# One core, packed attention and two gated expert layers: p, k, v attention in front for the first pair of batches alone, the other twelve units between the first pair's expert products

## The chip, the cores and the metric

One core of a Trainium2 chip runs the whole program; nothing is shared with other cores. The metric is the device time in microseconds (us), the median over runs of the same kernel. Five engines work in order, each on its own queue of instructions: TensorE (PE, with its weight loads as PEld), VectorE (DVE), ScalarE (ACT), GpSimd (POOL), and SyncE (SP), whose queue here issues every DMA.

## The reference

Eight batches of eight heads, 576 positions, head size 64, and 32 packed positions `p` per head:

```python
p_packed = sm_attn(p, k, v)                 # 32 packed rows look at 576 keys
out = sm_attn(q, p_packed, p_packed)        # 576 queries look at the 32 packed rows
x = out.transpose(0, 2, 1, 3).reshape(4608, 512)
g = x @ w_gate                              # 512 -> 1536
x = (silu(g) * (x @ w_val)) @ w_out         # 1536 -> 512
a, b = x @ w1, x @ w2                       # 512 -> 1024
return ((a * b) @ w3) @ w_out2              # 1024 -> 1024 -> 512
```

`sm_attn` is a softmax with the maximum taken off and a scale of 1/8. The weights arrive as float64 and are turned into float32 on the chip.

## The kernel before, in words

**Units.** A unit `u` is one batch and half of its heads (four heads), so there are 16. For each unit the first attention runs through `pa_kT` (k and p are transposed on TensorE, ScalarE copies them out), `pa_s` (scores, and VectorE takes their maximum), `pa_exp` (ScalarE), `pa_T` (the exponentials are transposed), `pa_P` (times v, VectorE divides) and `pa_PT` (the packed result is transposed into `PT0` for the first pair of batches, into `PTh` and `PTl` for the later ones).

**Pairs.** Batches are taken in four pairs P. For a pair and each of 12 slices f of the 1536 expert columns, `c_mm` multiplies the packed rows by the slice of `w_gate` and `w_val` (out: `ch`, `cl`, a number kept as two parts). `stage1` multiplies these by the second attention's weights (`aTh`, `aTl`, made by the `q_` functions), takes Silu on ScalarE and the product on VectorE, and splits it into `uh` and `ul`. After each three slices `stage3` multiplies them by `w_out` and adds to `acc`. `stage1` and `stage3` are the expert products that fill TensorE's time.

**Front.** All 16 units, the four q halves of the first pair (`q_rows` to `q_aT`), the conversion of the first weights (`w_conv`, `wo_conv`) and the first two `c_mm` stand ahead of the first `stage1`. The loop over s (L627) puts step s of unit s beside later steps of the units before it; a table (`extra`, L593 to L618) places the q halves and weights among them. This piece is in the written order on every engine. In the loop over pairs and slices (L878) the framework orders the instructions of each engine; that order is fixed once the program is built.

**Weights.** `conv` (L329) turns a raw float64 block into float32: one pass on ScalarE, two or three on VectorE. `raw_load` has three buffers. In pair 0 the slice f+3 of `w` and f+1 of `w_out` are converted while slice f is multiplied; the later pairs read the converted weights back.

**PSUM.** During the front, `psA` has three buffers of two banks and `psB` two of one bank. From slice 0 of pair 0 (`NPS = 0`) all eight banks are one pool `ps` with four buffers of two banks.

Of the kernel before, what the change touches and what calls it, by code (L numbers as in the profile page):

```python
# [16 lines left out]
M0 = None  # L17
KVB = 4
VB = 3
VD = 0  # L20
RAW0 = (2, 2, 4, 7, 10, 13, 14, 16, 17, 19)
WS = {5.0: (0, 0), 7.0: (0, 1), 8.0: (1, 0), 10.25: (1, 1), 15.75: (2, 0), 16.25: (2, 1)}
CVD = (0.25, 1.25)
SPD = 2.25
WO0 = 17.5
CS = (17, 18)
CO = (18.0, 19.0)
QS = (0, 1, 5, 6)
QD = ((0, 'load'), (4.0, 'T'), (5.25, 'mm'), (6.0, 'max'), (6.0, 'sub', 'pool'), (6.75, 'exp'), (7.25, 'sum'), (7.75, 'div', 'pool'), (8.75, 'aT', 'later'), (10.5, 'split'))
STD = 4.75  # L30
W3B = 5
DSIGN = ('w',)
SIGN = -(1 << 31)
W3S = ((0, 1, 2, 3), (1, 3), (1, 3))
NPS = 0
# [3 lines left out]
def packed_attention_moe_kernel(  # L39
# [84 lines left out]
    aA = pool("aA", "left")  # L124
    psA = tc.alloc_tile_pool(name="psA", bufs=3, space=bass.MemoryType.PSUM, reuse_waits="tile")
# [12 lines left out]
    a_pools = [aA, None]  # L138
    hs = [slice(32 * hq, 32 * hq + 32) for hq in range(4)]

    def q_load(b, Q):
        t = qp.tile([128, 2, NB32, 32], F32, tag="qr", name=f"qr{b}_{Q}")
        for i in range(4):
            for pr in range(2):
                nc.sync.dma_start(
                    t[32 * i:32 * i + 32, pr],
                    q[b, 4 * Q + 2 * pr + i // 2, :, 32 * (i % 2):32 * (i % 2) + 32].rearrange(
                        "(n t) d -> t n d", t=32),
                )
        q_t[b, Q] = t  # L150
# [15 lines left out]
    def q_rows(b, Q):  # L166
        t = qp.tile([128, NR, D], F32, tag="qr", name=f"qr{b}_{Q}")
        nc.sync.dma_start(t, q[b, 4 * Q:4 * Q + 4].rearrange("h (p r) d -> (h p) r d", r=NR))
        q_t[b, Q] = t

    def q_rT(b, Q):
        x = q_t.pop((b, Q))
        qT = qp.tile([128, NR // 2, 128], F32, tag="qT", name=f"qT{b}_{Q}")
# [5 lines left out]
        nc.vector.tensor_copy(qT[:, 0:8], t.rearrange("p a (m n) -> p (a m) n", n=128))  # L179
# [3 lines left out]
    def q_rmm(b, Q):  # L183
        qT, PTd = qT_t.pop((b, Q)), PTd_t.pop((b, Q))
        if Q == 0:
            sT_t[b] = qp.tile([128, 2, 2, HS], F32, tag="sT", name=f"sT{b}")
# [39 lines left out]
    def q_max(b, Q=None):  # L226
        sT, n, nj = q_view(b, Q)
        if not Q:
            sm_q[b] = (qp.tile([128, NJ, 1], F32, tag="qmx", name=f"qmx{b}"),
                       qp.tile([128, NJ, 1], F32, tag="qsm", name=f"qsm{b}"))  # L230
# [23 lines left out]
    def q_aT(b, Q, sub_on="dve"):  # L254
        at = a_pools[b // 2 % 2]
        if Q == 0:
            aT_t[b] = (at.tile([128, 2, 2, HS], F32R, tag=f"aTh{b % 2}", name=f"aTh{b}"),
                       at.tile([128, 2, 2, HS], F32R, tag=f"aTl{b % 2}", name=f"aTl{b}"))
        hi, lo = aT_t[b]
        sT = sT_t[b] if Q == 0 else sT_t.pop(b)  # L260
        aT = qp.tile([128, 2, HS], F32, tag="aT", name=f"aT{b}_{Q}")
        nc.vector.transpose(out=aT.rearrange("p a s -> p (a s)"),
                            in_=sT[:, Q].rearrange("p a s -> p (a s)"))
        if sub_on == "later":
# [3 lines left out]
            return conv_q.append(lambda: split(*by_row, src, sub_on="pool"))  # L268
        split(hi[:, Q], lo[:, Q], aT, sub_on=sub_on)

    def q_tasks(b, at, n):
# [46 lines left out]
    def raw_load():  # L318
        if raw_at[0] < len(raw_q):
# [4 lines left out]
            nc.sync.dma_start(t, src)  # L324
            raw_t.append((key, t))

    in_front, conv_rest = [True], []

    def conv(key, t):  # L329
# [13 lines left out]
        dve = not in_front[0] and key.startswith(DSIGN)  # L343
        sg = None if dve else vc.tile(list(t.shape), F32, tag="sg", name=f"sg_{key}")
        nc.vector.tensor_scalar(x, low, 29, None, op0=ALU.logical_shift_right)

        def sign():
            if not dve:
                nc.scalar.activation(sg, high.bitcast(F32), AF.Sign)

        def rest():
            nc.vector.scalar_tensor_tensor(
                x, t.bitcast(I32), 3, x, op0=ALU.logical_shift_left, op1=ALU.bitwise_or)
            if dve:
                nc.vector.scalar_tensor_tensor(
                    t.bitcast(I32), high, SIGN, x, op0=ALU.bitwise_and, op1=ALU.bitwise_or)
            else:
                nc.gpsimd.tensor_tensor(out=t, in0=x.bitcast(F32), in1=sg, op=ALU.mult)

        if in_front[0]:  # L360
            conv_rest.extend((sign, rest))
        else:
            sign()
            rest()
        if not in_front[0]:
            raw_load()
# [40 lines left out]
    wop = pool("wop", "right", bufs=4)  # L407
    cp = pool("cp", "right", bufs=2)
# [66 lines left out]
    def load_kv(u, nm):  # L475
# [30 lines left out]
    def pa_s(u):  # L506
# [10 lines left out]
        mx = pa.tile([128, 1], F32, tag="mx", name=f"mx{u}")  # L517
# [4 lines left out]
    def pa_exp(u, t, mx):  # L522
        a = pa.tile([128, NV, PK], F32, tag="ap", name=f"ap{u}")
# [7 lines left out]
    def pa_T(u):  # L531
# [8 lines left out]
        aT = pa.tile([PK, 2, 3, 128], F32, tag="apT", name=f"apT{u}")  # L540
# [3 lines left out]
    def pa_P(u):  # L544
# [9 lines left out]
        Pz = pa.tile([128, 2, 64], F32, tag="Pz", name=f"Pz{u}")  # L554
# [4 lines left out]
        if u < 4:  # L559
            Pd = pa.tile([128, 2, 64], F32, tag="Pd", name=f"Pd{u}")  # L560
# [4 lines left out]
    def pa_PT(u):  # L565
# [29 lines left out]
    def task(s, fn, *args):
        extra.setdefault(s, []).append((fn, args))

    for (b, Q), s in zip([(0, 0), (0, 1), (1, 0), (1, 1)], QS):
        for d, fn, *x in QD:
            task(s + d, {"load": q_rows, "T": q_rT, "mm": q_rmm, "max": q_max, "sub": q_sub, "exp": q_exp,  # L600
                         "sum": q_sum, "div": q_div, "aT": q_aT,
                         "split": lambda b, Q: conv_q.pop(0)()}[fn], b, Q, *x)
    for s in RAW0:
        task(s, raw_load)
    for s, (f, gv) in WS.items():
        task(s, w_conv, f, gv)
        for d in CVD:
            task(s + d, lambda: conv_rest.pop(0)())
        if gv == 1:
            task(s + STD, w_store, f)  # L610
    task(WO0, wo_conv, 0)
    for d in CVD:
# [499 lines left out]
```

## Time and profile before

| what | value |
|---|---|
| median of 3 runs | 1445.85 us (1436.72, 1446.46, 1445.85) |
| the profiled execution | 1441.93 us; its span is 1440.2 us |
| PE busy in the span | 1393.1 us (97%), 9960 instructions |
| DVE busy | 780.2 us (54%) |
| ACT busy | 642.5 us (45%) |
| POOL busy | 457.7 us (32%) |
| mean granted TensorE clock | 0.98 |
| DMA | 230.26 MB, mean 160 GB/s |

The busy shares are means over stretches with different limits. The profiled execution took 1441.93 us, of which 1440.2 us lie between its first and last instruction; it stands 3.9 us below the median of the runs. A line `L88` is a helper (`sub`) that many steps share, so its rows are told apart by the tiles they name. The span of a matmul in a row includes time in the pipeline; the distance of the starts is what TensorE takes.

### The profile page before, as it was taken

What the parts mean: (1) busy time and instruction counts of PE and PEld (TensorE: products, weight loads), DVE (VectorE), ACT (ScalarE), POOL (GpSimd) and SP (SyncE); (2) the same over time, 40 slices, a digit from 0 to 9 for tenths busy, and PEclk for the clock granted to TensorE, in tenths of its full rate; (3) what the DMA queues carried; (4) which work ended last, traced back from release to release, by engine and by line L of the source; (5) the groups of instructions that cost most, each with busy time, mean ns of one, the idle gap of its engine ahead of it and who ended that gap; (6) DMA issues with size and microseconds to landing.
All of it is one profiled execution on the core that took longest, in us unless ns stands there. A gap on an engine that the chain in (4) does not pass through costs nothing. (4 is left out here: it accounts for less than half of the span.)

```text
span 1440.2 us, 25384 instructions
## 1 busy us (share of the span) xinstructions
PE 1393.1 (97%) x9960; PEld 1302.1 (90%) x9960; DVE 780.2 (54%) x1188; ACT 642.5 (45%) x1077; POOL 457.7 (32%) x341
## 2 busy tenths in 40 slices
PE   7679999999999999999999999999999999999998
PEld 5457998999999999999989999989989899899997
DVE  3467798767875455756366647962333413334130
ACT  5575545536655355564464433643323323233231
POOL 0334133434544434455243223721202112021120
PEclk9888999999999999999999999999999999999999
DMA  9997575676533322215353324964827548275451
GB/s 270 239 248 205 163 210 188 160 237 166 165 83 83 117 60 70 66 53 176 96 157 100 131 72 174 339 242 154 256 75 236 179 133 253 92 223 180 133 168 44
DMA packets 175255, 230.26 MB, mean 160 GB/s; under 512 B 69408, under 2 KB 102176, under 8 KB 175136
## 3 DMA queue, kind: packets, MB, share of 16 engines
q1 hardware_dynamic: 175136, 228.64, 52.2%
q8 instruction: 79, 1.29, 0.4%
q14 instruction: 40, 0.33, 0.1%
HBM read 179.04 MB, written 49.55 MB: 159 GB/s over the span
## 5 line engine op out<-in xcount | busy, mean ns | idle before, releaser
L88 POOL TENSOR_TENSOR ul<-u,uh 128x576 fp32r<-128x576 f32 x96 | 145.4, 1519 | 247.7 <-ACT uh L92 247.3
L1005 POOL TENSOR_TENSOR c<-s,s 128x384 f32<-128x384 f32 x48 | 48.8, 1016 | 376.0 <-ACT s L1000 375.6
L701 PE MATMUL px<-ul,woh 128*128 128x288 f32 x768 | 165.3, 297 | 1.3 <-POOL ul L88 1.3
L701 PE MATMUL px<-uh,woh 128*128 128x288 f32 x768 | 165.4, 297 | 0.7 <-ACT uh L92 0.7
L701 PE MATMUL px<-uh,wol 128*128 128x288 f32 x768 | 164.9, 296 | 0.0
L1000 ACT COPY s<-pA 128x384 f32<-128x384 f32 x144 | 69.0, 479 | 181.1 <-PE pA L985 181.1
L88 DVE TENSOR_TENSOR cl<-pc,ch 64x512 fp32r<-64x512 f32 (+2 forms) x120 | 105.1, 900 | 55.4 <-ACT ch L455 47.6
L701 PEld LDWEIGHTS px<-uh,woh 128*128 128x128 f32 x768 | 124.1, 189 | 2.4 <-issue 1.4
L701 PEld LDWEIGHTS px<-ul,woh 128*128 128x128 f32 x768 | 124.3, 190 | 1.5 <-POOL ul L88 1.5
L701 PEld LDWEIGHTS px<-uh,wol 128*128 128x128 f32 x768 | 124.3, 189 | 0.0
L88 POOL TENSOR_TENSOR wl<-wf,wh 128x1024 fp32r<-128x1024 f32 x36 | 86.9, 2414 | 97.4 <-ACT wh L92 86.7
L1049 PE MATMUL po<-wo_hi,abl 128*128 128x512 f32 x288 | 112.2, 389 | 0.0
L1049 PE MATMUL po<-wo_lo,abh 128*128 128x512 f32 x288 | 112.1, 389 | 0.0
L1049 PE MATMUL po<-wo_hi,abh 128*128 128x512 f32 x288 | 112.0, 389 | 0.0
L711 DVE TENSOR_TENSOR acc<-acc,px 128x576 f32<-128x576 f32 x96 | 71.2, 746 | 66.1 <-PE px L701 65.9
L92 ACT CAST uh<-u 128x576 fp32r<-128x576 f32 x96 | 64.6, 674 | 93.5 <-DVE u L683 93.1
L88 DVE TENSOR_TENSOR abl<-ab,abh 128x768 fp32r<-128x768 f32 x48 | 48.6, 1013 | 105.2 <-ACT abh L92 105.2
L683 DVE TENSOR_TENSOR u<-u,pv 128x576 f32<-128x576 f32 x96 | 72.1, 751 | 48.8 <-PE pv L676 43.2
L88 POOL TENSOR_TENSOR wol<-wof,woh 128x512 fp32r<-128x512 f32 x48 | 66.9, 1406 | 88.3 <-ACT woh L92 80.7
L676 PE MATMUL pg<-aTh,ch 128*128 128x288 f32 x384 | 85.2, 304 | 4.8 <-DVE acc L711 3.3
L681 ACT ACTIVATE u<-pg 128x576 f32<-128x576 f32 x96 | 62.5, 651 | 49.4 <-PE pg L676 46.6
L676 PE MATMUL pg<-aTl,ch 128*128 128x288 f32 x384 | 83.3, 299 | 0.0
(362 smaller groups left out, 3544.1 us busy)
## 6 DMA issues: line engine op xcount, KB each, us to landing
ws<-wsd SPq DMA_DIRECT2D x245, 256.0 KB, 3.1
wf<-Wd SPq DMA_DIRECT2D x36, 512.0 KB, 3.4
raw_w<-in_moe_w_dram SPq DMA_DIRECT2D x32, 512.0 KB, 4.5
wsd<-ws SPq DMA_DIRECT2D x49, 256.0 KB, 4.0
raw_wo<-in_moe_w_out_dram SPq DMA_DIRECT2D x20, 512.0 KB, 4.4
km<-in_k_dram SPq DMA_DIRECT2D x16, 576.0 KB, 8.0
vm<-in_v_dram SPq DMA_DIRECT2D x16, 576.0 KB, 8.0
wof<-wod SPq DMA_DIRECT2D x36, 256.0 KB, 2.8
```

Source lines behind the costliest of these rows:

```text
L88: eng.tensor_tensor(out=out, in0=src, in1=hi.bitcast(F32), op=ALU.subtract)
L92: nc.scalar.copy(hi, src)
L676: nc.tensor.matmul(t[:, hf, 0:HS], lhsT=w[:, b % 2, Q, cols], rhs=x[:, Q, hf, :], start=first, stop=last,)
L681: nc.scalar.activation(u, t[:, :, 0:HS], AF.Silu)
L683: nc.vector.tensor_tensor(out=u, in0=u, in1=t[:, :, 0:HS], op=ALU.mult)
L701: nc.tensor.matmul(t[:, hf, 0:HS], lhsT=w[:, 128 * d:128 * d + 128], rhs=x[:, hf, :], start=first, stop=last,)
L711: nc.vector.tensor_tensor(out=o, in0=o, in1=t[:, :, 0:HS], op=ALU.add)
L1000: nc.scalar.copy(o, t)
L1005: on.tensor_tensor(out=r, in0=o, in1=t, op=op)
L1049: nc.tensor.matmul(t, lhsT=a[:, j, cols], rhs=w[:, f], start=first, stop=last)
```

## The change

The first attention of units 0 to 3 (the first pair of batches) and the first pair's q halves stay in front, in an order written out call by call. The other twelve units are issued by `hook()`: it is called after each `stage1` of pair 0 and after each half of a `stage3` in pair 0, and alternates between two halves of a unit's steps. With it:

- `c_mm` of slices 0 (in front) and 1 (ahead of the first `stage1`) come as before, weights of slices 0 and 1 are converted in front, and slice f+2 is converted while slice f is multiplied (before: f+3).
- In the front, the sign of a converted weight is put in by a third pass on VectorE, not by ScalarE and GpSimd.
- `psA` and `psB` (three buffers of two banks, two of one) stay until slice 10 of pair 0 (`NPS = 10`).
- In every pair, `stage3` of the first batch stands ahead of `stage1` of the next slice (before: behind it); the pools for `u`, k and the second attention's weights are shared or smaller (`up` has 6 buffers for 7).
- The q loads of the later pairs are kept behind the weight load issued before them.

```diff
-NPS = 0
+NFU = 4
+NPS = 10
 ...
+    with tc.manual_schedule(engines=M0):
+        load_p(0)
+        load_kv(0, "k")
+        load_kv(1, "k")
+        load_kv(0, "v")
+        q_rows(0, 0)
 ...
+        front_q(1, 0, "mm")
+        pa_PT(3)
+        front_q(1, 1, "T")
+        c_mm(0, 0)
+        front_q(1, 0, "exp")
+        front_q(1, 1, "mm")
+        w_conv(1, 0)
+        front_q(1, 0, "sum")
+        front_q(1, 1, "exp")
+        front_q(1, 0, "aT")
+        front_q(1, 1, "sum")
+        w_conv(1, 1)
 ...
+    def hook():
+        i, odd = divmod(hook_n[0], 2)
+        hook_n[0] += 1
+        u = NFU + i
 ...
+        if not odd:
+            if on(u):
+                if u % 2 == 0:
+                    twice_p(u // 2)
+                    if u // 2 + 1 < B:
+                        load_p(u // 2 + 1)
+                pa_kT(u)
+                load_kv(u + 3, "k")
+            if on(u - 1):
+                pa_T(u - 1)
+            if on(u - 2):
+                pa_PT(u - 2)
+        else:
+            if on(u):
+                front_s(u)
+            if on(u - 1):
+                pa_P(u - 1)
+                load_kv(u + 1, "v")
 ...
@@ stage3
+            if d % 2 == 1 and P == 0:
+                hook()
@@ the loop over pairs and slices
-        if n > 0 and at(1) is not None:
+        if at(1) is not None:
             c_mm(*at(1))
 ...
+        if pend is not None:
+            stage3(*pend, 0)
+        stage1(2 * P, f)
+        if P == 0:
+            hook()
 ...
+        if pend is not None:
+            stage3(*pend, 1)
+            pend = None
+        stage1(2 * P + 1, f)
+        if P == 0:
+            hook()
```

**The end of the front on TensorE.** Here `pc0_0` and `pc0_1` are the first two `c_mm`, `pg0_0` the first `stage1`; `pat`, `pP`, `pPT` are steps of the units. Before:

```order
L424 MATMUL pc0_0_1568<-wf0_0_452,PT0_79 64x256 x8
L537 MATMUL pat15_1579<-ident_66,ap15_1521 96x128 x6
L551 MATMUL pP14_1588<-vm14_1330,apT14_1519 32x64 x24
L570 MATMUL pPT14_1621<-ident_66,Pz14_1613 128x128
L424 MATMUL pc0_1_1627<-wf0_1_753,PT0_79 64x256 x8
L551 MATMUL pP15_1636<-vm15_1411,apT15_1586 32x64 x24
L570 MATMUL pPT15_1672<-ident_66,Pz15_1661 128x128
L676 MATMUL pg0_0_1702<-aTh0_824,ch0_0_1617 128x288 x2
```

With the change:

```order
L176 MATMUL pqr1_1_596<-ident_66,qr1_1_266 128x128
L402 MATMUL pc0_0_608<-wf0_0_454,PT0_79 64x256 x8
L192 MATMUL psq1_1_622<-qT1_1_594,PTd3_591 32x288 x8
L475 MATMUL pkr4_748<-ident_66,zp2_570 128x128
L478 MATMUL pkr4_748<-ident_66,km4_566 128x128
L475 MATMUL pkr5_888<-ident_66,zp2_570 128x128
L402 MATMUL pc0_1_698<-wf0_1_635,PT0_79 64x256 x8
L696 MATMUL pg0_0_712<-aTh0_403,ch0_0_617 128x288 x2
```

The first expert product no longer follows unit 15 but the last q half of the first pair and `c_mm` of slice 1.

**What `c_mm` of slice 1 waits for on VectorE, with the change.** `wf0_1` is its weight; `qsm1` and `aT1_0` belong to the softmax of the second batch's q halves.

```order
L263 STREAM_TRANSPOSE aT1_0_650<-sT1_572 128x576
L245 TENSOR_REDUCE qsm1_585<-sT1_572 128x18
L246 TENSOR_SCALAR qsm1_585<-qsm1_585 128x18
L247 RECIPROCAL qsm1_585<-qsm1_585 128x18
L341 TENSOR_SCALAR vx_w_1_1_658<-raw_w_1_1_460 128x512
L342 SCALAR_TENSOR_TENSOR vx_w_1_1_658<-wf0_1_635,vx_w_1_1_658 128x512
L344 SCALAR_TENSOR_TENSOR wf0_1_635<-raw_w_1_1_460,vx_w_1_1_658 128x4x128
```

The weight's last pass stands behind the second batch's softmax; before, that weight was ready among the units of the front.

**Slice 1 on ScalarE.** `ch0_2` is the copy of `c_mm` for slice 2, `u0_1` and `u1_1` are the Silu of the two batches, `ap4` is the exponential of unit 4. Before:

```order
L448 CAST ch0_2_1814<-pc0_2_1805 128x1024
L342 ACTIVATE wof0_2_1867<-raw_wo_2_1756 128x512
L681 ACTIVATE u0_1_1818<-pg0_1_1819 128x576
L92 CAST uh0_1_1847<-u0_1_1818 128x576
L92 CAST woh0_2_1924<-wof0_2_1867 128x512
L681 ACTIVATE u1_1_1876<-pg1_1_1877 128x576
```

With the change:

```order
L504 ACT_TABLE_LOAD
L504 ACTIVATE ap4_834,sm4_835<-psp4_822,mx4_831 128x2x3x96
L340 ACTIVATE wof0_1_780<-raw_wo_1_683 128x512
L423 CAST ch0_2_850<-pc0_2_841 128x1024
L701 ACT_TABLE_LOAD
L701 ACTIVATE u0_1_854<-pg0_1_855 128x576
L83 CAST woh0_1_837<-wof0_1_780 128x512
L340 ACTIVATE wf0_3_915<-raw_w_3_0_770 128x4x128
L83 CAST uh0_1_883<-u0_1_854 128x576
L481 COPY kT5_887<-pk5_890 128x1024
L520 COPY apT4_913<-pat4_906 96x768
```

Each unit adds an exponential, a table load ahead of it and one behind it (ahead of the next Silu), and five copies. Up to the last Silu of pair 0 the list has 24 table loads; before it had 6.

## Rows read from the trace of the kernel before

**Rows 1.** Windows: busy us of each engine (count), granted clock, DMA share, GB/s.
```profile
0.00:40.00 40.00, 30.39 (x454) 22.26 (x454) 16.76 (x55) 20.61 (x40) 2.46 (x12) 0.91 0.96 265
80.00:100.00 20.00, 17.16 (x394) 12.29 (x392) 12.03 (x43) 16.30 (x35) 8.25 (x6) 1.00 1.07 282
0.00:119.40 119.40, 85.14 (x1432) 60.80 (x1433) 61.62 (x190) 68.19 (x140) 27.83 (x33) 0.86 0.92 244
119.40:298.00 178.60, 178.55 (x1362) 165.42 (x1363) 145.73 (x207) 91.25 (x132) 68.71 (x43) 0.99 0.66 188
298.00:1440.00 1142.00, 1129.36 (x7168) 1075.88 (x7167) 572.83 (x794) 483.05 (x805) 361.11 (x266) 1.00 0.46 147
```
The engines stand in the order PE, PEld, DVE, ACT, POOL.

**Rows 2.** Waits of PE: us in total, times, longest; 0 to 120, then 120 to 920.
```profile
PE pat L537 <- DVE qT L179: 9.7, 2, 9.2
PE pPT L570 <- DVE Pz L556: 5.2, 4, 2.8
...
PE pg L676 <- DVE acc L711: 3.3, 1, 3.3
```

**Rows 3.** Timeline of PE: start, duration, instruction, count.
```profile
90.53 0.33 PE L496 MATMUL pkr<-ident,zp 128*128 128x128 f32 x1
...
94.14 0.33 PE L496 MATMUL pkr<-ident,zp 128*128 128x128 f32 x1
...
119.42 0.82 PE L676 MATMUL pg<-aTh,ch 128*128 128x288 f32 x2 [1.43 <-DVE cl L88]
...
191.32 1.95 PE L424 MATMUL pc<-wf,PT 128*64 128x256 f32 x16
```

**Rows 4.** Groups by shape on ACT, 0 to 120: count, busy us, mean ns.
```profile
L502 ACT COPY kT<-pk 128x1024 f32<-128x1024 f32 x16 | 16.2, 1011 | 16.0 <-PE pk L499 16.0
L541 ACT COPY apT<-pat 96x768 f32<-96x768 f32 x16 | 13.1, 816 | 10.0 <-PE pat L537 9.7
L525 ACT ACTIVATE ap<-psp,mx 128x576 f32<-128x576 f32 x16 | 11.9, 745 | 5.3 <-DVE mx L519 4.5 <-PE pk L499 0.8
L580 ACT CAST PTh<-pPT 128x64 fp32r<-128x64 f32 x24 | 4.0, 224 | 3.1 <-PE pPT L570 3.1
```

**Rows 5.** The same on DVE, 0 to 120.
```profile
L518 DVE TENSOR_REDUCE mx<-psp 128x1 f32<-128x576 f32 x16 | 11.8, 739 | 12.6 <-PE psp L514 12.6
L556 DVE SCALAR_TENSOR_TENSOR Pz<-pP,sm,mask 128x64 f32<-128x64 f32 x32 | 7.5, 277 | 6.2 <-PE pP L551 6.2
L352 DVE SCALAR_TENSOR_TENSOR vx_w<-wf,vx_w 128x512 int32<-128x512 int32 x7 | 5.3, 760 | 0.0
L245 DVE TENSOR_REDUCE qsm<-sT 128x18 f32<-128x576 f32 x4 | 3.0, 749 | 0.7 <-ACT sT L240 0.7
```

**Rows 6.** Window of slices 5 and 6 of pair 0; columns as in rows 1.
```profile
174.37:191.32 16.95, 16.95 (x129) 14.98 (x129) 16.71 (x25) 11.28 (x17) 7.57 (x4) 1.00 0.77 235
```

**Rows 7.** Timeline of DVE: unit 0's maximum, and `cl` of the `c_mm` at 191.32.
```profile
10.50 0.76 DVE L518 TENSOR_REDUCE mx<-psp 128x1 f32<-128x576 f32 x1 [8.84 <-PE psp L514]
...
199.71 1.21 DVE L88 TENSOR_TENSOR cl<-pc,ch 128x1024 fp32r<-128x1024 f32 x1
```

**Rows 8.** Timeline of ACT around two table loads.
```profile
122.18 1.28 ACT L681 ACT_TABLE_LOAD   x1
123.47 0.65 ACT L681 ACTIVATE u<-pg 128x576 f32<-128x576 f32 x1
...
244.18 0.65 ACT L681 ACTIVATE u<-pg 128x576 f32<-128x576 f32 x1
244.84 1.28 ACT L240 ACT_TABLE_LOAD   x1
```

**Rows 9.** DMA issues of the whole run: count, KB each, median us to landing.
```profile
raw_w<-in_moe_w_gate_dram SPq DMA_DIRECT2D x12, 512.0 KB, 4.5
km<-in_k_dram SPq DMA_DIRECT2D x16, 576.0 KB, 8.0
```

**Rows 10.** The page's costliest groups: busy us, mean ns, idle before, releaser.
```profile
L88 POOL TENSOR_TENSOR ul<-u,uh 128x576 fp32r<-128x576 f32 x96 | 145.4, 1519 | 247.7 <-ACT uh L92 247.3
```

More of the change, by code (lines that the diff above doesn't have):

```diff
@@ L17 @@
 M0 = None
[L18 to L30, printed above, removed]
+NFU = 4
+QS = (0, 1, 2, 3)
+QD = ((4.0, 'T'), (5.25, 'mm'), (6.0, 'max'), (6.0, 'sub', 'pool'), (6.75, 'exp'), (7.25, 'sum'), (7.75, 'div', 'pool'), (8.75, 'aT'), (9.5, 'split'))
+WS = {2.0: (0, 0), 3.5: (0, 1), 7.0: (1, 0), 8.0: (1, 1)}
+WO0 = 9.0
+NPS = 10
 W3B = 5
-DSIGN = ('w',)
 SIGN = -(1 << 31)
 W3S = ((0, 1, 2, 3), (1, 3), (1, 3))
-NPS = 0
 @with_exitstack
@@ L149, in q_load @@
                 )
+                if sp_last:
+                    tc.add_manual_dep(x.ins, sp_last[0].ins.name, NO_SYNC, reason="q behind the loads before it")
         q_t[b, Q] = t
@@ L166, in q_rows @@
     def q_rows(b, Q):
-        t = qp.tile([128, NR, D], F32, tag="qr", name=f"qr{b}_{Q}")
+        at = qp if b and Q else pf
+        t = at.tile([128, NR, D], F32, tag="qr", name=f"qr{b}_{Q}", bufs=1 if at is qp else 3)
         nc.sync.dma_start(t, q[b, 4 * Q:4 * Q + 4].rearrange("h (p r) d -> (h p) r d", r=NR))
@@ L185, in q_rmm @@
         if Q == 0:
-            sT_t[b] = qp.tile([128, 2, 2, HS], F32, tag="sT", name=f"sT{b}")
+            sT_t[b] = (pf if b else qp).tile([128, 2, 2, HS], F32, tag="sT", name=f"sT{b}", bufs=1)
         t = psum(f"psq{b}_{Q}")
@@ L342, in conv @@
         nc.scalar.activation(t, high.bitcast(F32), AF.Copy, scale=2.0 ** -112)
-        dve = not in_front[0] and key.startswith(DSIGN)
-        sg = None if dve else vc.tile(list(t.shape), F32, tag="sg", name=f"sg_{key}")
         nc.vector.tensor_scalar(x, low, 29, None, op0=ALU.logical_shift_right)
[L347 to L366, printed above, removed]
+        nc.vector.scalar_tensor_tensor(
+            x, t.bitcast(I32), 3, x, op0=ALU.logical_shift_left, op1=ALU.bitwise_or)
+        nc.vector.scalar_tensor_tensor(
+            t.bitcast(I32), high, SIGN, x, op0=ALU.bitwise_and, op1=ALU.bitwise_or)
+        raw_load()
     W_t, wf_t, wst_t = {}, {}, {}
@@ L522, in pa_exp @@
     def pa_exp(u, t, mx):
-        a = pa.tile([128, NV, PK], F32, tag="ap", name=f"ap{u}")
+        a = at_home(u, pf, "ap", vl, "wf", [128, NV, PK], f"ap{u}")
         sm = pa.tile([128, 1], F32, tag="sm", name=f"sm{u}", bufs=3)
@@ L559, in pa_P @@
         if u < 4:
-            Pd = pa.tile([128, 2, 64], F32, tag="Pd", name=f"Pd{u}")
+            Pd = pf.tile([128, 2, 64], F32, tag="Pd", name=f"Pd{u}")
             for e in range(2):
@@ L603, in packed_attention_moe_kernel @@
[L603 to L612, printed above, removed]
-        task(WO0 + d, lambda: conv_rest.pop(0)())
-    task(WO0 + STD, wo_store, 0)
-    C_t["later"] = [None]
-    for f in range(2):
-        task(CS[f] + 0.5, c_mm, 0, f)
-        task(CO[f], lambda: c_out(*C_t["later"].pop(1)))
@@ L650, in packed_attention_moe_kernel, with front_q @@
-    assert not extra, extra
-    C_t.pop("later")
-    pa.release()
-    psB.release()
-    in_front[0] = False
-    psC = tc.alloc_tile_pool(name="psC", bufs=1, space=bass.MemoryType.PSUM, reuse_waits="tile")
-    ps_at.append(psC)
-    aB = pool("aB", "right")
-    a_pools[1] = aB
-    up = pool("up", "right", bufs=7)
+    def front_q(b, Q, what):
+        for fn in {"T": [q_rT], "mm": [q_rmm, q_max, lambda b, Q: q_sub(b, Q, "pool")], "exp": [q_exp],
+                   "sum": [q_sum, lambda b, Q: q_div(b, Q, "pool")],
+                   "aT": [lambda b, Q: q_aT(b, Q, True)]}[what]:
+            fn(b, Q)
```

235 lines of the change are left out of this document (129 added, 106 removed).

## The prediction

> **What bounds the kernel now.** I read the windows first. From 119.4 us on TensorE is never short of work: it is busy 178.55 of the 178.6 us of pair 0 and 1129 of the 1142 us behind it, at a granted clock of 0.99 and 1.00 [rows 1]. The list of waits says the same: between 120 and 920 us its longest wait is one of 3.3 us [rows 2]. So the end is set by TensorE's work plus whatever time it lacks work, and most of the latter lies in the front: 85.14 us busy of 119.4, clock 0.86 [rows 1]. There it waits for copies on VectorE, 9.7 us in two waits and 5.2 in four [rows 2], while the DMA engines are 0.92 busy at 244 GB/s [rows 1]: 16 units' k and v (576 KB each [rows 9]) have to arrive ahead of the first expert product, which starts at 119.42 us [rows 3]. The timeline of TensorE gives the price of a unit when nothing is missing: from one unit's first transpose to the next one's it takes 94.14 - 90.53 = 3.61 us [rows 3].
>
> **The front gets shorter.** What stays ahead of the first product is units 0 to 3, the four q halves of the first pair, the weights of slices 0 and 1, and two `c_mm`.
> By bytes: 8 k and v transfers and 4 q transfers of 0.59 MB and two weight blocks of 0.52 MB come to 8.1 MB, 31 us at the 265 GB/s of the first 40 us [rows 1]. That is not the last thing to be ready. `c_mm` of slice 1 stands ahead of the first product on TensorE and needs the last pass of its weight, which on VectorE stands behind the softmax of all four q halves. From unit 0's maximum, at 10.50 us [rows 7], to that pass VectorE has 64 rows. By the same instructions before [rows 5] they are: four units at 2.3 us (maximum 0.74, four products of 0.28, small ones 0.46), four q halves at about 4.2 (two reductions of 0.75 among them) less one transpose, four conversions at 2.0 (three passes, the second 0.76), one copy of 1.2; together 34 us. ScalarE's list up to there is 34 us too.
> Ends: without any wait VectorE is through at 10.5 + 34 = 44.5 us; at the share it had in the whole front, 61.62 of 119.4, it needs 34 / 0.516 = 66 us and is through at 76. I take the densest window of that front, 80 to 100 us, which had its data: ScalarE 0.82 busy, VectorE 0.60 [rows 1]. 34 us of work take 41 us at the one and 57 at the other; the middle, 49, gives 59.5 us. `c_mm` of slice 1 then takes 1.95 [rows 3], so the first product starts near 61.5.
> One more wait follows. The last block of slice 2's weight can be loaded only when slice 1's conversion has given its buffer back; 4.5 us to landing [rows 9], a pass on ScalarE, the copy of slice 1's `c_mm` and a table load of 1.28 [rows 8] stand ahead of the first Silu, about 9 us in all, and TensorE has only some 6 us of work until it needs a PSUM buffer. I add 2.5 and count the dense part from 64. Gain: 119.4 - 64 = 55.4 us (ends 73 and 38).
>
> **Twelve units come back.** They take TensorE's own time now: 12 x 3.61 = 43.3 us. Nothing hides that; TensorE is full there.
>
> **What the other engines make of it.** In the steps without a `stage3` (slices 1, 2, 4, 5, 7, 8) the window of two slices shows TensorE 16.95 us, VectorE 16.71, ScalarE 11.28 [rows 6]. Two units are added. TensorE: 16.95 + 7.22 = 24.2 us. VectorE gets 2.2 us a unit (maximum, two products of 0.28, two PTl parts, small ones): 21.1, or 87%. ScalarE gets per unit 1.01 + 0.38 + 0.95 + 0.82 + 0.45 = 3.6 us of copies and the exponential [rows 4], and two table loads of 1.28 because exponential and Silu now alternate: 11.28 + 7.2 + 5.1 = 23.6 us, or 98% of TensorE's time. DMA: 235 GB/s for 16.95 us is 4.0 MB; two more units make 6.4 MB in 24.2 us, 263 GB/s, what the front reached [rows 1]. All fit, barely, and only if none waits for another. The slices with a `stage3` have room on every engine but TensorE.
> Before, such a lag cost nothing: the second part of the copy for the `c_mm` at 191.32 us came only at 199.71 [rows 3, 7], and TensorE did not wait. That was with four double buffers in PSUM; now there are three until slice 10, shared with the units' transposes and scores, and the weights are converted one slice less ahead. Ends: 0 us, as before; and all of a unit's chain from scores to exponential uncovered, 0.74 + 0.15 + 1.28 + 0.95 = 3.1 us, for 12 units 37 us. I take 10 us, some 3.3 for each of the three pairs of slices: nearer the low end, since the row of two slices had VectorE at 16.71 of 16.95 without a wait.
> The table load shows no tail: Silu starts at 123.47, 0.01 us behind the load's end, and a load starts at 244.84, 0.01 us behind the Silu ahead of it [rows 8]. The Trainium skill, "ScalarE: Activation LUTs", section "What ACT_TABLE_LOAD costs", puts a switch at 1283 ns for the load and about 1380 ns more for a drain. The load agrees with the row; the drain is not in it, and the sum goes by the row.
>
> **Behind pair 0.** `stage3` of a first batch now starts one `stage1` sooner after its last operand. That chain is Silu, 0.65 [rows 8], a product and a cast of the same shape, some 0.7 each, and GpSimd's difference, 1.52 [rows 10]: 3.6 us. The other batch's `stage1` covers it but for 0.3 (half of a slice's 16.95 / 2 - 1.95 = 6.5 us [rows 3, 6]), and `c_mm` and the first matmuls of the group, which need older slices, cover the rest. I count 0; if a queue eats the cover, 16 groups at half a microsecond make +8; the 3.3 us wait of [rows 2] may vanish, -3.
>
> **Sum.** Against the profiled execution: 1441.9 - 55.4 + 43.3 + 10 + 0 = 1439.8 us. The profiled execution is 3.9 us below the median of the runs shown, 1445.85, of which one took 1436.72; I name 1440 and leave it at that. What can be told from no change here is 1%, 14.5 us: below 1431.4 is faster, above 1460.3 slower.
>
> **Rivals.**
> *The units are hidden well and the front is dense.* VectorE runs the front almost without waits (through near 47 us, counted from 50 with the wait behind it: gain 69), and three buffers suffice (3 us). 1441.9 - 69 + 43.3 + 3 = 1419. For it: VectorE kept TensorE fed while 99% busy [rows 6]. Against it: the q halves are a chain over five engines, and no window of the front had VectorE above 0.6 for long. Chance 0.25, 1415 to 1428.
> *Evacuation becomes the bound: slower.* The place is PSUM in slices 1 to 9. A score buffer is held until its maximum, a table load and the exponential are done, behind `c_mm`'s copies; with three buffers TensorE meets it two tiles later. At 3.1 us a unit, 37 us: 1441.9 - 55.4 + 43.3 + 37 = 1467. It decides for slower from 32 us, 2.6 a unit. For it: ScalarE at 98% by the sum above. Against it: the absorbed lag of 8 us [rows 3, 7]. Chance 0.16, 1455 to 1475.
> *ScalarE is the bound through table switches alone.* Were a switch to hold ScalarE for the load's length once more (the engine empty between), two slices would take it 11.28 + 7.2 + 10.2 = 28.7 us against TensorE's 24.2, 4.5 us more for three pairs of slices on top of the 10: about 1453. [rows 8] speak against it: neither side of a load has such a gap. The page's drain is the rule behind this rival. Chance 0.07, 1447 to 1458.
>
> **Chances and range.** My forecast, 0.52, has 1428 to 1452 for itself; a tenth of it lies below 1431.4. Faster by over 1%: 0.25 + 0.05 = 0.30. Slower by over 1%: most of the evacuation case and a little of front and lag adding up, 0.14. Within 1%: 0.56. The range for 8 in 10 leaves out the outer half of each end case: 1419 to 1463.
>
> **What would show it.** The first expert product near 61 us, with a wait at the second or third tile behind it; twelve groups of transposes and scores between products up to slice 9; the end of pair 0 some 2 us sooner than before (12 less the 10 of waits). In the waits of TensorE, ScalarE (Silu, exponential, copies) and VectorE named in slices 1, 2, 4, 5, 7, 8 and little in 3 and 6. I would be wrong if the front ended beyond 72 us, if TensorE's waits in pair 0 came to over 20 us or under 3, or if the time behind pair 0 moved by more than 5.

## The result, and the profile after

The changed kernel takes 1464.12 us (median of four runs, 1463.92 to 1466.94), the kernel before 1445.76 beside it: ratio 1.0147, 95% interval 1.0111 to 1.0182. It is slower by 1.5%, where 1440 us was forecast, with a chance of 0.56 on a time within 1% of before.

Three stretches of the profiled execution answer to [rows 1]: up to the first expert product, from there to pair 1's first `c_mm`, and the rest. Columns as there.

With the change:

```profile
0.00:63.37 63.37, 34.79 (x463) 23.23 (x464) 36.09 (x86) 30.06 (x49) 18.93 (x23) 0.84 0.67 197
63.37:296.30 232.93, 208.12 (x2155) 179.59 (x2154) 158.53 (x297) 141.54 (x222) 55.43 (x40) 0.95 0.70 209
296.30:1465.20 1168.90, 1152.26 (x7346) 1096.45 (x7344) 575.55 (x809) 497.35 (x821) 373.39 (x273) 1.00 0.46 145
```

The first two of these stretches in the kernel before:

```profile
0.00:119.42 119.42, 85.14 (x1432) 60.82 (x1433) 61.64 (x190) 68.19 (x140) 27.85 (x33) 0.86 0.92 244
119.42:274.31 154.89, 154.89 (x1185) 142.02 (x1186) 132.19 (x189) 79.81 (x116) 56.79 (x36) 0.99 0.68 193
```

The front gave 119.42 - 63.37 = 56.0 us, pair 0 took back 232.9 - 154.9 = 78.0, and the rest is 1168.9 for 1165.9 (+3.0): 25.0 us more in the spans (1465.2 for 1440.2). The medians differ by 18.4, since the execution profiled after stands 2.8 above its median and the one before 3.8 below.

TensorE's timeline at the end of the front (start, duration, instruction, count, idle ahead and its releaser):

```profile
60.16 3.29 PE L402 MATMUL pc<-wf,PT 128*64 128x256 f32 x16 [7.45 <-DVE wf L344]
63.37 0.53 PE L696 MATMUL pg<-aTh,ch 128*128 128x288 f32 x2
...
67.66 0.33 PE L478 MATMUL pkr<-ident,km 128*128 128x128 f32 x1 [0.83 <-DMA km<-in_k_dram]
69.66 0.65 PE L478 MATMUL pk<-ident,km 128*128 128x128 f32 x2 [1.67 <-DVE cl L79]
```

In pair 0, where TensorE never waited before, the list of its waits (us in total, times, longest) now begins so, from 62 to 297 us:

```profile
PE psq L208 <- DVE qT L155: 4.9, 2, 3.4
PE pPT L549 <- DVE Pz L535: 4.7, 4, 2.1
PE pk L478 <- DVE cl L79: 4.6, 4, 1.7
PE psq L208 <- DVE PT L160: 3.2, 2, 2.7
PE pg L696 <- DVE cl L79: 2.4, 1, 2.4
PE pat L516 <- ACT u L701: 1.3, 1, 1.3
```

Most end on VectorE (2.9 us end on ScalarE, 0.8 on a load), which is busy 68% of that stretch: it is late, not full. The longest one shows how; TensorE first, VectorE second:

```profile
248.52 0.88 PE L530 MATMUL pP<-vm,apT 96*32 96x64 f32 x48
249.99 0.33 PE L549 MATMUL pPT<-ident,Pz 128*128 128x128 f32 x1 [0.60 <-DVE Pz L535]
253.68 1.84 PE L208 MATMUL psq<-qT,PT 128*32 128x288 f32 x16 [3.36 <-DVE qT L155]
```

```profile
249.47 0.47 DVE L535 SCALAR_TENSOR_TENSOR Pz<-pP,sm,mask 128x64 f32<-128x64 f32 x2
250.36 1.57 DVE L160 TENSOR_TENSOR PT<-PTh,PTl 128x64 f32<-128x64 f32 x2 [0.42 <-PE pPT L549]
251.85 0.34 DVE L79 TENSOR_TENSOR PTl<-pPT,PTh 128x64 fp32r<-128x64 f32 x2
252.11 1.42 DVE L155 STREAM_TRANSPOSE qT<-qr 128x576 f32<-128x576 f32 x2
```

A unit's product, its division, its transpose, then the q half's sum (which waits for the transpose, since `Pz` and `PT` share one buffer) and its transposes follow one another over two engines, with nothing placed between them on TensorE. The granted clock then falls: windows of 40, 20 and 40 us.

```profile
160.00:200.00 40.00, 35.80 (x364) 29.18 (x365) 34.44 (x66) 24.19 (x39) 6.65 (x5) 0.96 0.69 203
200.00:220.00 20.00, 20.00 (x262) 18.06 (x262) 8.71 (x23) 12.24 (x22) 5.01 (x4) 1.00 0.54 152
220.00:260.00 40.00, 30.75 (x316) 23.29 (x313) 32.74 (x62) 23.51 (x39) 7.66 (x6) 0.87 0.66 200
```

In the window in which TensorE was busy throughout, the clock is 1.00; in the one with 9.3 of 40 us empty it is 0.87 (a mixture of the levels 1.2 and 2.4 GHz).

### The profile page after: what moved, and what is told of

Read it like the earlier page. It is cut to its first block, busy times and chain, and to the rows that moved or that the text cites. A ratio compares the mean times of both kernels' runs of the same rounds, so it can differ in the third digit from the quotient of the medians.

```text
span 1465.2 us, 25374 instructions
## 1 busy us (share of the span) xinstructions
PE 1395.2 (95%) x9960; PEld 1299.3 (89%) x9960; DVE 770.2 (53%) x1191; ACT 669.0 (46%) x1092; POOL 447.8 (31%) x334
## 4 chain that ended last, share of the span: by engine, by line
PE 77%; DVE 8%; ACT 5%; DMA 4%; issue 4%; POOL 2%; SPq 0%; DVEq 0%; ACTq 0%; POOLq 0%
PE px L721 17%; PE pA L1012 14%; PE po L1076 13%; PE pB L1012 7%; PE pg L696 7%; PE pv L696 6%; PE pC L1012 3%; PE pc L415 2%; DVE cl L79 1%; DVE vx_w L342 1%; PE pc L402 1%; DVE u L703 1%; PE psq L208 1%; PE pk L478 1%; DMA raw_w<-in_moe_w_val_dram 1%
## 5 line engine op out<-in xcount | busy, mean ns | idle before, releaser
L79 POOL TENSOR_TENSOR ul<-u,uh 128x576 fp32r<-128x576 f32 x96 | 141.9, 1480 | 289.9 <-ACT uh L83 275.3
L79 POOL TENSOR_TENSOR wol<-wof,woh 128x512 fp32r<-128x512 f32 x48 | 62.8, 1322 | 127.1 <-ACT woh L83 127.1
L701 ACT ACTIVATE u<-pg 128x576 f32<-128x576 f32 x96 | 62.6, 652 | 72.2 <-PE pg L696 61.5
L696 PE MATMUL pv<-aTh,ch 128*128 128x288 f32 x384 | 82.9, 297 | 5.2 <-ACT u L701 4.3
```

Of the source, the lines that this page charges most:

```text
L79: eng.tensor_tensor(out=out, in0=src, in1=hi.bitcast(F32), op=ALU.subtract)
L696: nc.tensor.matmul(t[:, hf, 0:HS], lhsT=w[:, b % 2, Q, cols], rhs=x[:, Q, hf, :], start=first, stop=last,)
L701: nc.scalar.activation(u, t[:, :, 0:HS], AF.Silu)
```

## The experiments

One measure serves for all: the stretch from the loop's first `c_mm` (60.16 us in the changed kernel) to pair 1's first `c_mm`. The changed kernel takes 236.1 us for it: 24.8 with TensorE idle, and 211.3 busy. Of the busy time 201.5 is the work as priced (154.9, 3.3 for the `c_mm`, 43.3 for twelve units); the 9.8 left over are put down to the lower clock, 0.94 against 0.99 before. Each row is one profiled execution; beside them the kernel before took 1438 to 1448 us, so totals tell only some 10 us. No kernel has two traces, so how far its stretch scatters isn't known, and differences of two or three us in it mean little. "Rest" is the time behind the stretch; `nu` in a name says that units 4 to 15 are left out, and a total is given only where nothing was left out or replaced.

| run | stretch | idle in it | clock | rest | total |
|---|---|---|---|---|---|
| before (154.9 + 3.3) | 158.2 | 0 | 0.99 | 1165.9 | 1441.9 |
| changed | 236.1 | 24.8 | 0.94 | 1168.9 | 1466.9 |
| x1_no_units | 187.0 | 21.7 | 0.95 | 1173.8 | |
| x2_nu_psum4 | 176.4 | 14.5 | 0.98 | 1171.8 | |
| x2_nu_lead3 | 176.4 | 12.8 | 0.97 | 1168.5 | |
| x3_nu_both | 174.2 | 12.9 | 0.97 | 1170.8 | |
| y_nu_all | 173.0 | 11.9 | 0.97 | 1174.0 | |
| z_nu_noq | 164.6 | 9.8 | 0.99 | 1171.7 | |
| x1_no_q1 | 212.7 | 14.1 | 0.98 | 1174.7 | |
| x1_no_switch | 226.9 | 16.9 | 0.95 | 1165.1 | |
| x1_no_sign | 230.0 | 18.9 | 0.94 | 1174.0 | |
| x2_psum4 | 240.0 | 24.3 | 0.93 | 1178.9 | 1481.9 |
| x2_lead3 | 237.0 | 24.0 | 0.93 | 1166.6 | 1466.3 |
| x2_qapart | 229.5 | 23.3 | 0.96 | 1182.0 | 1473.5 |
| y_all | 223.2 | 15.8 | 0.96 | 1174.3 | 1460.3 |
| x3_spread | 220.3 | 23.9 | 0.95 | 1198.7 | 1481.4 |
| x3_spread_l3q | 214.6 | 21.6 | 0.95 | 1193.8 | 1470.6 |

The rest moves between 1165 and 1179 where nothing in it was edited. TensorE's order there is the same in x1_no_units and x2_lead3 as in the changed kernel, while VectorE's and ScalarE's differ shortly behind pair 0; how much of the 14 us that makes was not tested. One part is more regular: from the first product with `w1` (`pA`) to the end, the five kernels with a buffer of its own for `Pz` and the smaller mask (x2_psum4, x2_qapart, y_all and both x3_spread) take 556.4 to 557.5 us, all others 551.1 to 553.6. No unit runs there, so about 5 us of these five rests and totals belong to that edit itself, in a way that stays open.

**Are the units the cause?**

```diff
 def hook():
     ...
+    return
```

> Left out: units 4 to 15 (their loads and all their steps; PTh and PTl are filled with a constant). The loop order, the three PSUM buffers until slice 10, the weights converted two slices ahead and pair 1's q halves stay as in the changed kernel. There, from the first c_mm of the loop (60.2 us) to pair 1's first c_mm (296.3 us) it took 236 us with 24.8 us of TensorE idle and a granted clock of 0.95; the kernel before took 155 from its first product. Theory (the units beside the products make the stalls): the stretch falls to about 158 us, TensorE idle in it under 4 us, clock 0.99. Rival (loop order, fewer PSUM buffers or the later conversion stall by themselves): 165 us or more, idle 8 us or more.

187.0 us with 21.7 idle: the rival. Twelve units account for 49.1 of the 78; 28.8 are lost by the loop without any unit. Windows and waits of this kernel:

```profile
60.55:247.50 186.95, 165.29 (x1200) 148.55 (x1201) 149.93 (x201) 85.21 (x123) 56.97 (x37) 0.95 0.65 191
```

```profile
PE pg L695 <- DVE cl L79: 9.9, 2, 6.9
PE psq L210 <- DVE qT L157: 4.1, 2, 2.4
PE px L720 <- DVE cl L79: 2.1, 2, 1.9
PE pv L695 <- DVE sT L217: 2.0, 1, 2.0
```

**What does the loop lack?** The same without units, with two slacks of the kernel before put back, alone and together.

```diff
-NPS = 10
+NPS = 0
```

> Left out: units 4 to 15, as in x1_no_units, and beside that the four shared double buffers of PSUM start at slice 0 as in the kernel before. x1_no_units took 187.0 us from the loop's first c_mm to pair 1's, 28.8 more than the 158.2 (154.9 + 3.3) of the kernel before, with 21.7 us of idle on TensorE, of which 12.9 stand behind the difference cl, that is behind a buffer of PSUM or the tile itself. Theory (three double buffers let VectorE's lag through): 160 to 168 us, idle under 8. Rival (the lag is that of the conversions, one slice later, and of the q halves): over 178 us.

```diff
-        if at(2) is not None and at(2)[0] == 0:
-            w_conv(at(2)[1], 0)
+        for i in (2, 3) if n == 0 else (3,):
+            if at(i) is not None and at(i)[0] == 0:
+                w_conv(at(i)[1], 0)
 ...
```

> Left out: units 4 to 15, as in x1_no_units, and beside that slice f+3 is converted while slice f is multiplied, as in the kernel before (slices 2 and 3 while slice 0 is). Theory (PSUM): 180 to 190 us from the loop's first c_mm to pair 1's, idle 15 to 25. Rival (the later conversion is what stalls): 160 to 170 us, idle under 8.

Both gave 176.4, 10.6 less each: neither range of either run held it. Either slack helps, and neither is the whole. The two windows, and then the one with both slacks:

```profile
60.87:237.30 176.43, 161.90 (x1201) 143.40 (x1201) 147.81 (x201) 83.78 (x121) 54.97 (x36) 0.98 0.66 196
61.20:237.60 176.40, 163.65 (x1201) 144.99 (x1202) 142.42 (x201) 84.78 (x123) 56.16 (x37) 0.97 0.67 196
61.28:235.50 174.22, 161.31 (x1200) 143.47 (x1201) 143.94 (x201) 84.74 (x123) 56.90 (x37) 0.97 0.66 198
```

> Left out: units 4 to 15, as in x1_no_units (187.0 us from the loop's first c_mm to pair 1's). Both edits together: four shared double buffers of PSUM from slice 0, and slice f+3 converted while slice f is multiplied; each alone gave 176.4. Theory (two slacks of the kernel before that the change gave up, each covering a part of its own): 164 to 168 us, idle under 6. Rival (either one covers the same lag, the rest comes from the order and the q halves): 173 to 177 us.

174.2: together 12.8, hardly more than one alone. They cover the same lag, as the rival had it. Then the q halves of pair 1: their products one slice later (`q_mm` called in the next slice), or the halves left out of pair 0.

> Left out: units 4 to 15. With four shared double buffers of PSUM from slice 0, the conversion three slices ahead, and in pair 0 the q products one slice behind their transposes. x3_nu_both, the same with the products directly behind, took 174.2 us from the loop's first c_mm to pair 1's, with 7.8 us of psq waits. Theory (the q products' place is half of the 16 us left): 163 to 168 us, psq waits under 2. Rival (the waits move on, as with the units): 171 to 176 us.

> Left out: units 4 to 15, and the four q halves of pair 1 in pair 0 (their weights are a constant set by GpSimd); four double buffers and the conversion three slices ahead as in x3_nu_both (174.2 us). The halves take 4.7 us of TensorE. Theory (with all slack put back, what stalls is the q halves): 154 to 161 us, idle under 4, which is the 158.2 of the kernel before less the halves' work and a little. Rival (the order of stage3 and the start of pair 0 stall by themselves): 164 to 170 us.

Moved, they gave 1.2 us (one wait of 6.8 for `qT` took the place of the others: the rival). Left out, 9.6 less than x3_nu_both, of which 4.7 are their work: at 164.6 us with 9.8 idle this is the lower end of the rival's 164 to 170, and not the theory's 154 to 161 with under 4. In this last kernel the whole stretch and a window near its start are:

```profile
61.23:225.80 164.57, 154.79 (x1137) 140.93 (x1138) 124.04 (x167) 76.32 (x116) 57.21 (x37) 0.99 0.66 208
80.00:100.00 20.00, 17.68 (x131) 15.17 (x130) 19.72 (x25) 10.00 (x17) 7.81 (x6) 1.00 0.80 265
```

and of its 9.8 us of idle 5.6 lie in five waits before 95 us, where VectorE is full (19.72 of 20): it converts slices 2 and 3 there, the first of which the kernel before had converted in its front.

**Parts of the change put into the kernel before.** There the stretch is 154.9 us.

```diff
@@ y_b_order
+        if pend is not None:
+            stage3(*pend, 0)
         stage1(2 * P, f)
@@ y_b_q
-            1: lambda: (q_T(b, 0), q_load(b, 1)),
-            2: lambda: (q_mm(b, 0), q_T(b, 1)),
+            1: lambda: (q_T(b, 0), q_mm(b, 0), q_load(b, 1)),
+            2: lambda: (q_T(b, 1), q_mm(b, 1), q_max(b), q_sub(b)),
@@ y_b_oqp: both, and
-    ps_at.append(psC)
-NPS = 0
+NPS = 10
```

> The kernel before, with one part of the change: in every pair stage3 of a batch stands ahead of that batch's stage1 of the next slice. The kernel before takes 154.9 us from its first product to pair 1's first c_mm and 1165.9 us from there to the end. Theory (the order takes the cover from uh and ul and costs a part of the 16 us): 158 to 168 us, and 2 to 8 us more behind pair 0. Rival (VectorE's lag is absorbed by four PSUM buffers in either order): 154 to 157 us, under 2 more behind.

> The kernel before, with one part of the change: the q products of the later pairs directly behind their transposes, in slices 3, 4, 8 and 9. Theory (psq then waits for VectorE, as in the kernel changed without units, 4 to 8 us): 159 to 166 us for the 154.9. Rival (harmless while no unit stands beside): 154 to 157 us.

> The kernel before, with three parts of the change: stage3 first, the q products directly behind their transposes, and three double buffers of PSUM until slice 10. Theory (these and the later conversion are what costs 28.8 us in the loop without units): 170 to 182 us for the 154.9. Rival (the loss needs the new front or the later conversion): 154 to 162 us.

156.3 (rest 1177.1), 157.5 (rest 1165.5) and 166.8 (rest 1165.3). In pair 0 each is nearly free alone, 1.4 and 2.6 us, at its rival's 154 to 157 or half a microsecond above; with three buffers the three cost 11.9, between the ranges of theory and rival, and more than the two together.

```profile
114.96:281.80 166.84, 157.95 (x1191) 143.64 (x1186) 138.35 (x198) 82.92 (x122) 58.90 (x37) 0.98 0.66 192
```

The 11 us behind pair 0 in y_b_order don't appear in y_b_oqp, which has the same order of `stage3` and `stage1`, so they can't be put on that order alone.

**The same slack with the units in.** x2_psum4 shares four double buffers from slice 0 (and gives `Pz` its own buffer, with room from a smaller mask), x2_lead3 converts f+3, x2_qapart calls `q_mm` a slice later; y_all has all three (`q_mm` later in pair 0 alone).

```diff
@@ x2_psum4
-NPS = 10
+NPS = 0
 ...
+        if len(ps_at) == 1:
+            return psum(name)[:, 0]
         return psB.tile([128, 512], F32, tag="B", name=name)
 ...
-    Pz = at_home(u, vl, "vu", qp, "PT", [128, 2, 64], f"Pz{u}")
+    Pz = at_home(u, vl, "vu", pa, "Pz", [128, 2, 64], f"Pz{u}")
@@ x2_qapart
-            1: lambda: (q_T(b, 0), q_mm(b, 0), q_load(b, 1)),
-            2: lambda: (q_T(b, 1), q_mm(b, 1), q_max(b), q_sub(b)),
+            1: lambda: (q_T(b, 0), q_load(b, 1)),
+            2: lambda: q_T(b, 1),
```

> The changed kernel with four shared double buffers of PSUM from slice 0 on (the units' small tiles take a double buffer too), and a buffer of its own for the units' Pz, without which this order locks up. The stretch from the loop's first c_mm to pair 1's was 236.1 us. Theory (PSUM is what lets VectorE's lag through): 205 to 218 us, idle under 10, total 1436 to 1447. Rival (units, q halves and conversions stall each other through VectorE whatever the buffers): 226 to 240 us.

> The changed kernel, with slice f+3 converted while slice f is multiplied (slices 2 and 3 while slice 0 is); nothing is left out. Theory (the loop's lost slack stalls with the units as without them): the stretch of 236.1 us falls by about 10, to 222 to 230, total 1450 to 1458. Rival (with units in between, their chains stall first, as the four PSUM buffers showed): 232 to 240 us.

> The changed kernel with the q products (psq) of the later pairs called one slice behind their transposes on VectorE, as in the kernel before, and a buffer of its own for the units' Pz; three double buffers of PSUM stay. x1_no_q1 took 23 us off the stretch of 236.1 us, of which only 4.7 are work. Theory (psq waits because it stands directly behind its transposes): the 8.1 us of psq waits fall below 2, with the lower clock behind them, stretch 220 to 226. Rival (the q halves cost by VectorE's time and PSUM buffers, wherever they stand): 231 to 238.

> The changed kernel with its units, and four shared double buffers of PSUM from slice 0, slice f+3 converted while f is multiplied, the q products of pair 0 one slice behind their transposes, and Pz with its own buffer. The stretch from the loop's first c_mm to pair 1's was 236.1 us; 240.0, 237.0 and 229.5 with one of these each. Theory (the chains of units, q halves and conversions each stall as soon as another is cured; together they free TensorE): 212 to 224 us, total 1440 to 1452. Rival (with units the waits move on whatever slack is given): 227 to 242 us, total 1455 to 1470.

Alone +3.9, +0.9 and -6.6: with units in, two of three do nothing (their rivals), and x2_qapart lies between its two ranges. In x2_psum4 the waits only change their names:

```profile
PE pk L480 <- DVE cl L79: 7.4, 4, 2.6
PE psq L210 <- DVE qT L157: 5.9, 2, 3.8
PE psq L210 <- ACT ap L506: 3.3, 1, 3.3
PE pg L698 <- ACT kT L483: 3.1, 3, 2.6
```

In x2_qapart the psq waits fell from 8.1 to 5.7 us, not below 2, and one new wait of 8.2 us for `cl` came up at the end of pair 0. Together -12.9 us, idle 15.8: 223.2 is the upper end of the theory's range, but the rest grew by 5 (nearly all of it behind the first `pA`), and the total of 1460.3 is the rival's. No version here beats the kernel before.

These pairs also show that the price of the twelve units depends on the loop they stand in. With and without units the stretch differs by 49.1 us in the changed kernel (236.1 and 187.0), by 63.6 with four PSUM buffers (240.0 and 176.4), by 60.6 with the earlier conversion (237.0 and 176.4), and by 50.2 with all three slacks (223.2 and 173.0); the kernels with units have the `Pz` edit in the second and the last of these pairs. Their work is 43.3, so the stalls that go with them are 6 to 20 us: "the loop's" and "the units'" stalls don't simply add up.

**What do single loads on the engines cost?** Left out in turn: pair 1's q halves in pair 0, Silu (a copy for it), the sign pass.

```diff
@@ x1_no_q1
+            if P:
+                q_tasks(2 * P + 2, 2, f)
+                q_tasks(2 * P + 3, 6, f)
@@ x1_no_switch
-                nc.scalar.activation(u, t[:, :, 0:HS], AF.Silu)
+                nc.scalar.activation(u, t[:, :, 0:HS], AF.Copy if b < 2 else AF.Silu)
@@ x1_no_sign
-        nc.vector.scalar_tensor_tensor(
-            t.bitcast(I32), high, SIGN, x, op0=ALU.bitwise_and, op1=ALU.bitwise_or)
```

> Left out: the four q halves of pair 1 in pair 0 (their second attention weights are a constant set by GpSimd); the units stay. In the changed kernel waits of psq on qT and PT are 8.1 of the 24.8 us of TensorE idle in pair 0, and psq itself takes 4.7 us. Theory (q halves and units collide on VectorE): end of the stretch 296.3 falls to about 275 to 280: 4.7 of work, 8 of waits, and most of the 10 us at the lower clock, since the waits at 145, 162, 236 and 254 us stand where the clock fell. Rival (one wait takes the place of the other, the units' own chain is long enough): falls by 5 to 9 us, idle still 18 us or more.

> Changed: in pair 0 a plain copy stands for Silu, so that exponential and Silu do not alternate and the table loads of pair 0 fall away (18 more of them than before, 23 us of ScalarE). ScalarE is 61 per cent busy in pair 0 of the changed kernel. Theory (data chains over VectorE, little on ScalarE): pair 1's first c_mm at 296.3 moves by 0 to 6 us. Rival (table switches delay the exponential and the copies, as the rival on ScalarE in the prediction has it): it moves by 12 us or more, to 284 or sooner.

> Left out: the third pass on VectorE (the sign) of the weights converted in the loop, 30 passes or about 22 us of VectorE's 160 in pair 0. Theory (the stalls are chains through VectorE's queue, so less in front of a copy or product there shortens them): idle of 24.8 falls by 5 to 10 us and the end at 296.3 by 8 to 15. Rival (PSUM or ScalarE): under 4 us.

-23.4, -9.3 and -6.1 us of the stretch. The q halves are 4.7 us of work and cost 18.7 more beside the units, against 4.9 more without them (in z_nu_noq, with both slacks back): the theory. Leaving them out also takes 23.4 us off VectorE's busy time, so this run can't tell their place from their load. The waits that are left stand on other tiles:

```profile
61.18:273.90 212.72, 198.61 (x2106) 175.35 (x2107) 137.87 (x265) 136.05 (x217) 59.85 (x44) 0.98 0.73 225
```

```profile
PE pv L696 <- ACT ap L504: 5.0, 5, 1.6
PE pk L478 <- DVE cl L79: 4.7, 5, 1.7
```

Table switching lies between theory and rival. Leaving out the sign pass takes 24 us off VectorE's busy time and 6 off the idle, within the theory's 5 to 10; the end of the stretch came only 4.2 us sooner (292.1), between the theory's 8 to 15 and the rival's under 4.

**Fewer units in pair 0.** Units 12 to 15 go to pair 2, the other eight spread over ten slices; x3_spread_l3q has f+3 and the later `q_mm` as well.

```diff
-        if P == 0:
+        if P == 0 or (P == 2 and f):
             hook()
 ...
+        if P == 2 and f == 0:
+            second_phase()
```

> The changed kernel with units 12 to 15 moved from pair 0 to pair 2, where VectorE and ScalarE are idle about half of the time, and the other eight called after each stage1 of pair 0 alone, so that they spread over ten slices; Pz has a buffer of its own. Theory (pair 0 stalls since its slices hold more chains than their buffers absorb; pair 2 has room): units 12 to 15 cost pair 2 their 14.4 us of TensorE and at most 3 more; pair 0 loses 14.4 of work and 8 to 15 of waits and low clock; total 1447 to 1457. Rival (the loop's own lost slack is nearly all of it): total 1459 to 1466.

> x3_spread with two things put back as in the kernel before: slice f+3 converted while slice f is multiplied, and in pair 0 the q products one slice behind their transposes. Theory (each is a part of its own): 8 to 18 us less than x3_spread, total 1432 to 1447, stretch of pair 0 with under 10 us of idle. Rival (the stalls only move to the next tile): within 5 us of x3_spread.

Pair 0 lost 15.8 us, just the four units' work and 1.4 of waits, and the rest grew by 29.8: at 1481.4 us x3_spread is outside both ranges. Of the 29.8, 25.1 lie ahead of the first `pA`, against 14.4 of work for four units; the other 4.8 are found in every kernel with the `Pz` edit. TensorE's idle time in the rest grew by only 5.3 (21.9 for 16.6). So the theory's price of at most 3 us for the move was not met, but with a rest that scatters as said above the 25.1 are no measure of a unit's stalls. The two slacks took 10.8 off x3_spread's total, within the 8 to 18 forecast, but 5.7 of it in pair 0, whose idle stayed at 21.6 (forecast under 10), and 4.9 in the rest, which is inside its scatter; 1432 to 1447 was missed.

## Why the prediction was wrong, step by step

- **The front** held. The first `c_mm` of the loop was forecast for 59.5 and started at 60.16, behind the last pass of its weight on VectorE, as the prediction said; VectorE had 33.3 us busy up to there (forecast 34). That the middle between two windows' shares hit was luck. The `c_mm` took 3.29 us, not 1.95: TensorE had been idle for 7.45, and its matmuls ran at the lower level. The wait counted behind it, 2.5 us, was 0.83 + 1.67, but not for the first Silu: one was for the k load of a unit, one for `cl`. The size was luck, and since these 2.5 lie inside pair 0's 78.0 us, the first product came at 63.37 for the forecast 61.5. The sum of bytes is short, too: slices 0 and 1 have four weight blocks of 0.52 MB, not two, so 9.2 MB and 35 us, which still was not the bound.
- **Twelve units at 3.61** held. TensorE's busy time grew by 46.0 us with them (211.3 for 165.3), 43.3 forecast. With 0, 8 and 12 units in pair 0 the stretch is 187.0, 220.3 and 236.1: 4.2 each for the first eight, 4.0 for the rest, 49.1 in all with their waits.
- **What the other engines make of it** is the step that failed: 10 us forecast (12.5 with the wait counted at the front), 78.0 - 43.3 = 34.7 measured. It priced what units add to a loop that it took for the one before ("Before, such a lag cost nothing"; lower end "0 us, as before"). Three PSUM buffers and one slice less of conversion stand in the same paragraph, and neither got a price. Without any unit the loop already loses 28.8 us, and the units add 5.9 to that. Of the 28.8, 12.8 come back with these two slacks and 4.9 more go with the q halves, beyond their work; 11.1 remain, 9.8 of them idle in z_nu_noq (5.6 of these at the start, where VectorE catches up with conversions). What makes the rest of these 11 wasn't settled: the new front, the order of `stage3` (1.4 us in the kernel before) and the smaller pools are in it, and the pools were not tried alone. The split holds for the changed kernel as it stands; with one slack put back the units' stalls are 17 to 20 us instead of 5.9. The prediction's own sign of being wrong, waits of over 20 us in pair 0, came true.
- **The low clock** had no term. With 24.8 us of idle the stretch is 34.6 longer than the work as priced; the 9.8 between them are put down to the lower level behind the waits (0.94 granted, 0.99 before).
- **Where**: the waits were expected in the slices without `stage3`, from ScalarE and VectorE alike. They stand mostly on VectorE. 8.1 of the 24.8 us are at the q halves, in slices 3, 4, 7 and 8 (the expectation of y_b_q names 8 and 9 for the last two), the longest 2.73 and 3.36 in slices 7 and 8; the prediction did not name the q halves at all.
- **The table load**: 23 loads in the stretch at 1283 ns, as [rows 8] and the forecast of 24. Without Silu no load is left in the stretch, ScalarE is busy 29.2 us less, and the stretch fell by 9.3 us. Behind every one of the 23 loads the next instruction starts after 0.01 us, and 13 loads start 0.02 us behind the instruction ahead of them. The Trainium skill, "ScalarE: Activation LUTs", section "What ACT_TABLE_LOAD costs", adds about 1380 ns of drain to a switch; these rows show none. So the rival that lets a switch hold ScalarE for twice the load is not borne out.
- **The rival "evacuation becomes the bound"** has the time, 1467, but not the mechanism: four PSUM buffers did not help with the units in (240.0 us), and its price per unit was 3.1 us where 5.9 / 12 = 0.5 were measured (1.7 with four buffers). Its limit for slower is 30.5 us, 2.5 a unit, by its own sum (1460.3 - 1441.9 + 55.4 - 43.3), not 32.
- **Behind pair 0**, 0 forecast between -3 and +8: +3.0, inside the scatter of the rest.

## What to carry to other kernels

When a change lets work into a loop that is full, first price the loop itself: every buffer, lead and distance that it gives up to make room, as a term, even where each is nearly free alone. Here the changed loop lost 29 us before any work was added to it, and two of these slacks were 13 of them. An engine that is well below full (VectorE, 68% busy) still stalls the one that waits for it in order: count dependent steps between two neighbouring instructions of the bound engine, not busy shares. Putting back one slack at a time can show nothing while several are missing, and what the added work costs has to be measured in the loop in which it will stand.

## What the runs showed of the hardware

VectorE's passes over two operands in SBUF stretch when they start while GpSimd works on a difference in SBUF. In x1_no_units, VectorE, then GpSimd:

```profile
233.62 2.85 DVE L344 SCALAR_TENSOR_TENSOR vx_w<-w12t,vx_w 128x512 int32<-128x512 int32 x1 [1.43 <-ACT w12t L342]
236.51 0.69 DVE L346 SCALAR_TENSOR_TENSOR w12t<-raw_w,vx_w 128x512 int32<-128x512 int32 x1
237.12 1.22 DVE L79 TENSOR_TENSOR cl<-pc,ch 128x1024 fp32r<-128x1024 f32 x1
```

```profile
233.59 2.34 POOL L79 TENSOR_TENSOR wl<-wf,wh 128x1024 fp32r<-128x1024 f32 x1
```

The pass takes 2.85 us for its usual 0.69: it ends 0.54 us behind GpSimd's instruction, which began 0.03 us before it. `cl` behind it came late, and TensorE waited 6.94 us, of which the stretched pass is 2.2. It is no single case: of the 152 such conversion passes of the changed kernel (L342 and L344) 35 began during a two-operand GpSimd instruction, and each of these ended 0.55 us behind it; the other 117 took 0.65 to 0.70 us, also where GpSimd began in the middle of them. The 1.57 us of the two small sums at 250.36 above (0.41 elsewhere) stand beside a GpSimd difference from 250.30 to 251.71. The Trainium skill, "SBUF — State Buffer", section "SBUF: two separate sides", says that a VectorE instruction with two SBUF inputs and a GpSimd instruction that reads SBUF exclude each other for a whole instruction; on VectorE's side these rows agree.
